# A convolution's backward pass: transposing the gradient in contiguous blocks with a DMA scatter, and leaving out two rows of zeros

## The chip, the cores and the metric

The kernel runs on one core of one Trainium2 chip. The metric is the device time of that core in microseconds (us). "PE" in the profile is TensorE, "PEld" its weight loads, "DVE" VectorE, "ACT" ScalarE, "POOL" GpSimd, "SP" SyncE. L445 is line 445 of the kernel. A line of a group reads: line, engine, operation, tiles (out<-in), shapes, count | busy time in us, mean ns of one | idle time before it and what ended it; a line of a timeline: start, duration, then the same. "From start to start" is the time from the first instruction of a group to the first of the next: matmuls overlap (those of L466 last 273 ns each by the page and are 109.3 ns apart from start to start), so this, and not their durations, adds up to the time. An eviction is the copy of a result out of the PSUM tile that TensorE wrote. The runs were made on several chips of the kind, on which the kernel before took 2769.7 to 2773.3 us, so kernels are compared by their ratio to the kernel before on the same chip. A ratio is the mean time of one kernel's fast runs over that of the other's of the same rounds, so it is not quite the ratio of the medians that are quoted.

## The reference

A strided 1-D convolution (31 taps, stride 2, 256 channels in and out), a normalisation over time per channel, a GELU; the kernel returns the output and all gradients.

```python
B, T, D, K = 2, 16000, 256, 31
L = (T - K) // 2 + 1                                   # 7985
h = sum over i of  x[:, i:i + 2*L:2, :] @ w[i]         # 31 matmuls per output
h = (h - mean_l(h)) / sqrt(var_l(h) + 1e-5) * gn_gamma + gn_beta
out = gelu(h)                                          # tanh form
# returned: out, and by jax.vjp with grad_out: grad x, grad w, grad gn_gamma, grad gn_beta
```

## The kernel before

It runs in stages: forward of both batches (up to some 930 us); transposing the weights while VectorE and ScalarE do the elementwise backward of the second batch (up to 1102); the layout stage; gradient of x (up to 1880); gradient of w (up to 2750). After the elementwise stage the gradient lies in `gu` as channels x time. The gradient of w needs it as time x channels, in `gQ`: partition q holds times 64 q to 64 q + 63. So the layout stage transposes, for each r in 0..63, the 125 columns r, r + 64, r + 128, ...:

```python
R = 64; NQ = 125; NR = R
# phase_gq(b, gate): layout stage
for zr in (0, NR + 1):                                  # a row of zeros before and after
    nc.scalar.activation(out=gQv[:, zr, :], ..., scale=0.0, bias=gate)
for r0 in range(0, NR, 4):
    ptr = ptr_tile()                                    # one PSUM tile, no second buffer
    for rr in range(4):
        r = r0 + rr
        for dc in range(2):
            nc.tensor.transpose(out=ptr[0:NQ, rr * 2 + dc, :],                              # L445
                                in_=guv[:, dc, bass.DynSlice(HALO + r, NQ, step=R)], identity=ident)
    gated_copy(ci % 2 == 1, gQv[0:NQ, 1 + r0:1 + r0 + 4, :], ptr[0:NQ, ...], gate)   # ACT or DVE in turn
```

`gate` is a zero that is known only when the elementwise stage is done. The gradient of w takes two taps (ih, il = ih - 2) at once: one matmul 512 wide with two neighbouring rows of gQ. For r = -1 and r = 63 one of the two rows is a row of zeros.

```python
# phase_bwd_w: gradient of w
for u in range(u_lo, u_hi + 1, 2):                      # u_lo starts at ih - 2
    for pi, (ih, il) in enumerate(pairs):
        r = (u - ih) // 2                               # -1 .. 63
        nc.tensor.matmul(accs[pi][:, 0:2*D], lhsT=chunk[0:nq_u, kk, cc*P:(cc+1)*P],  # L534
                         rhs=gQv[0:nq_u, 1 + r:3 + r, :], start=..., stop=...)
# the end, second batch: load the first batch's partial sum, add, store
for pi, (ih, il) in enumerate(pairs):
    res16 = gwpool.tile(..., name="gwres", bufs=2);  prev = gwpool.tile(..., name="gwprev", bufs=2)
    nc.gpsimd.dma_start(out=prev, in_=gw_scr[...]); nc.vector.tensor_tensor(out=res16, in0=prev, in1=accs[pi], op=ALU.add)
    nc.gpsimd.dma_start(out=out_2[ih, ...], ...);   nc.gpsimd.dma_start(out=out_2[il, ...], ...)
```

## Time and profile before

Median 2769.75 us of 4 runs (2769.6 to 2770.21).

| stage | from, us | to, us | what fills TensorE |
|---|---|---|---|
| forward, two batches | 0 | 931 | L234, 512 wide |
| weights transposed, elementwise stage | 935.0 | 1102 | L598, L380, early blocks of L466 |
| layout | 1102 | 1187.2 | L445, with L466 between |
| gradient of x | 1187.2 | 1880.0 | L466, 256 wide |
| gradient of w | 1880.0 | 2750.2 | L534 512 wide, L539 256 wide |
| end | 2750.2 | 2767.9 | nothing |

Read a row of the profile by its stage: busy time counts in full where TensorE is dense, and may cost nothing where it waits anyway. The lines are in the prediction.

### The profile page before, as it was taken

What the parts mean: (1) busy time and instruction counts of PE and PEld (TensorE: products, weight loads), DVE (VectorE), ACT (ScalarE), POOL (GpSimd) and SP (SyncE); (2) the same over time, 40 slices, a digit from 0 to 9 for tenths busy, and PEclk for the clock granted to TensorE, in tenths of its full rate; (3) what the DMA queues carried; (4) which work ended last, traced back from release to release, by engine and by line L of the source; (5) the groups of instructions that cost most, each with busy time, mean ns of one, the idle gap of its engine ahead of it and who ended that gap; (6) DMA issues with size and microseconds to landing.
All of it is one profiled execution on the core that took longest, in us unless ns stands there. A gap on an engine that the chain in (4) does not pass through costs nothing.

```text
span 2767.9 us, 38654 instructions
## 1 busy us (share of the span) xinstructions
PE 2712.7 (98%) x17351; PEld 1676.5 (61%) x17444; DVE 450.5 (16%) x1105; ACT 402.2 (15%) x785; POOL 263.3 (10%) x464
## 2 busy tenths in 40 slices
PE   8999999999999999999999999999999999999997
PEld 4444445444444678998888888885444454444443
DVE  1000000993000398100000000000000000000000
ACT  1000001964000575200000000000000000000000
POOL 2000000111000011011111111110000000011001
PEclk9999999999999999999999999999999999999998
DMA  5000000112000221000000000002333333333332
GB/s 161 16 24 16 24 13 24 43 53 60 24 16 13 75 72 39 8 18 21 21 21 20 20 20 21 21 21 60 120 99 94 96 119 102 103 114 118 104 109 83
DMA packets 214554, 152.89 MB, mean 55 GB/s; under 512 B 11268, under 2 KB 201392, under 8 KB 214388
## 3 DMA queue, kind: packets, MB, share of 16 engines
q1 hardware_dynamic: 189988, 95.32, 11.6%
q0 software_dynamic: 20368, 53.06, 5.3%
q8 instruction: 136, 2.23, 0.4%
q10 hardware_dynamic: 4032, 2.03, 0.2%
q14 instruction: 30, 0.25, 0.0%
HBM read 113.62 MB, written 36.75 MB: 54 GB/s over the span
## 4 chain that ended last, share of the span: by engine, by line
PE 88%; DVE 8%; ACT 1%; issue 1%; DMA 1%; POOL 0%; SPq 0%; POOLq 0%; ACTq 0%; DVEq 0%
PE acc L534 30%; PE acc L466 27%; PE acc L234 26%; PE ptx L445 2%; DVE etmp L364 1%; DVE gu L366 1%; DVE etmp L368 1%; PE acc L539 1%; DVE etmp L361 1%; PE ptx L196 1%; DVE gu L425 1%; DVE etmp L360 1%; DVE etmp L363 1%; PE pte L312 1%; DMA xn<-in_x_dram 1%
## 5 line engine op out<-in xcount | busy, mean ns | idle before, releaser
L466 PE MATMUL acc<-wB,gu 128*128 128x256 bf16 (+1 forms) x7812 | 870.4, 273 | 1.2 <-issue 1.2
L534 PE MATMUL acc<-gQ,xqc 125*128 125x512 bf16 (+1 forms) x3900 | 870.0, 379 | 0.0
L234 PE MATMUL acc<-xw,w_sb 128*128 128x512 bf16 (+1 forms) x3875 | 860.9, 375 | 6.1 <-issue 1.1
L466 PEld LDWEIGHTS <-gu 128*128 128x128 bf16 (+1 forms) x7812 | 769.4, 99 | 89.4 <-issue 2.9
L534 PEld LDWEIGHTS <-xqc 125*128 125x128 bf16 (+1 forms) x3900 | 380.6, 98 | 434.8 <-issue 0.2
L234 PEld LDWEIGHTS <-w_sb 128*128 128x128 bf16 x3968 | 375.7, 97 | 413.0 <-issue 2.5
L480 POOL DMA_DIRECT2D out_dram<-gxs x252 | 136.0, 540 | 786.6 <-ACT gxs L476 389.0
L478 DVE CAST gxs<-acc 128x256 bf16<-128x256 f32 (+1 forms) x126 | 53.4, 424 | 658.3 <-PE acc L466 656.7
L476 ACT CAST gxs<-acc 128x256 bf16<-128x256 f32 (+1 forms) x126 | 46.7, 371 | 657.6 <-PE acc L466 655.0
L241 ACT ACTIVATE hT<-acc 128x512 bf16<-128x512 f32 (+1 forms) x64 | 37.5, 587 | 651.1 <-PE acc L234 649.6
L200 DVE COPY xw<-ptx 128x1024 bf16<-128x1024 bf16 (+1 forms) x64 | 43.1, 673 | 544.7 <-PE ptx L196 544.7
L561 DVE TENSOR_TENSOR gwres<-gwprev,acc 128x512 bf16<-128x512 f32 (+1 forms) x32 | 20.6, 669 | 413.3 <-PE acc L534 352.8
L549 DVE COPY gwstg<-acc 128x512 f32<-128x512 f32 (+1 forms) x16 | 10.5, 658 | 432.4 <-PE acc L534 373.1
L549 ACT COPY gwstg<-acc 128x512 f32<-128x512 f32 x16 | 9.4, 585 | 436.2 <-PE acc L534 388.7
L391 POOL DMA_DIRECT2D out_dram<-ost x31 | 22.4, 724 | 529.2 <-ACT ost L388 472.7
L539 PE MATMUL acc<-gQ,xqc 125*128 125x256 bf16 x256 | 69.8, 273 | 0.0
L445 PEld LDWEIGHTS <-gu 128*125 128x125 bf16 x256 | 58.3, 302 | 1.3 <-issue 0.9
L555 POOL DMA_DIRECT2D gw_scr<-gwstg x32 | 17.2, 541 | 420.0 <-ACT gwstg L549 414.9
L445 PE MATMUL ptx<-ident,gu 128*125 128x128 bf16 x256 | 54.7, 358 | 1.0 <-DVE gQ L273 0.9
L565 POOL DMA_DIRECT2D out_dram<-gwres x32 | 17.3, 541 | 385.4 <-DVE gwres L561 334.6
L196 PE MATMUL ptx<-ident,xn 128*128 128x128 bf16 x496 | 39.7, 224 | 13.1 <-DMA xn<-in_x_dram 11.4
L353 ACT ACTIVATE etmp<-hT,vec 128x512 bf16<-128x512 bf16 (+1 forms) x64 | 51.2, 799 | 6.3 <-DVE etmp L364 6.0
(98 smaller groups left out, 929.5 us busy)
## 6 DMA issues: line engine op xcount, KB each, us to landing
xqc<-in_x_dram SPq DMA_DIRECT2D x120, 500.0 KB
out_dram<-gxs POOLq DMA_DIRECT2D x248, 64.0 KB, 1.8
xn<-in_x_dram SPq DMA_DIRECT2D x60, 256.0 KB
gnat<-in_grad_out_dram POOLq DMA_DIRECT2D x30, 256.0 KB, 3.1
gw_scr<-gwstg POOLq DMA_DIRECT2D x30, 256.0 KB, 5.6
gwprev<-gw_scr POOLq DMA_DIRECT2D x30, 256.0 KB, 5.6
xqc<-in_x_dram SPq DMA_DIRECT2D x16, 434.0 KB
out_dram<-ost POOLq DMA_DIRECT2D x31, 128.0 KB, 2.2
```

The source lines that it names most:

```text
L196: nc.tensor.transpose(out=ptr[:, bb * NCC + cc, :], in_=xn[:, bi0 + bb, cc * P:(cc + 1) * P], identity=ident[:, :])
L200: nc.vector.tensor_copy(out=dst, in_=src)
L234: nc.tensor.matmul(pst[:, 0:lw], lhsT=w_sb[:, cc, i, dc * P:(dc + 1) * P], rhs=xw[:, p, cc, j:j + lw], start=(k == 0), stop=(k == nmm - 1),)
L241: nc.scalar.activation(out=hTv[:, dc, l0:l0 + lw], in_=pst[:, 0:lw], func=ACT.Identity, accum_out=st.hsum[:, dc, wi:wi + 1])
L353: nc.scalar.activation(out=Tt[:, 0:cw], in_=hs, func=ACT.Square, bias=B_, scale=A_)
L445: nc.tensor.transpose(out=ptr[0:NQ, rr * NDC + dc, :], in_=guv[:, dc, bass.DynSlice(HALO + r, NQ, step=R)], identity=ident[:, :])
L466: nc.tensor.matmul(pso[0:mw, 0:D], lhsT=guv[:, dc, HALO + m0 - j:HALO + m0 - j + mw], rhs=wB[:, dc, i, :], start=(k == 0), stop=(k == nmm ...
L476: nc.scalar.copy(out=gxs[0:mw, :], in_=pso[0:mw, 0:D])
L478: nc.vector.tensor_copy(out=gxs[0:mw, :], in_=pso[0:mw, 0:D])
L480: nc.gpsimd.dma_start(out=dst, in_=gxs[0:mw, :])
L534: nc.tensor.matmul(accs[pi][:, 0:2 * D], lhsT=chunk[0:nq_u, kk, cc * P:(cc + 1) * P], rhs=gQv[0:nq_u, 1 + r:3 + r, :], start=st_flag, stop ...
L539: nc.tensor.matmul(accs[pi][:, 0:D], lhsT=chunk[0:nq_u, kk, cc * P:(cc + 1) * P], rhs=gQv[0:nq_u, 1 + r, :], start=st_flag, stop=sp_flag)
```

## The change

Its intent: read contiguous columns in the transposes, so that they cost what the contiguous transposes of L598 cost (55 ns each, beside 211), and let DMAs do the rearranging (a block of 128 times is two rows of gQ; each half of 64 partitions x 512 bytes is copied into one partition). Spread these sets among the blocks of the gradient of x in a fixed order, one set per six blocks after 48 blocks in free order. And multiply no row of zeros: the first row's second half becomes one 256-wide matmul of its own.

```diff
-        gQv = gQt[:, 0:(NR + 2) * D]...
-        for zr in (0, NR + 1): nc.scalar.activation(... zeros ...)
-        for r0 in range(0, NR, RPT): ...
-                    nc.tensor.transpose(out=ptr[0:NQ, ...], in_=guv[:, dc, bass.DynSlice(HALO + r, NQ, step=R)], ...)
-            gated_copy(ci % 2 == 1, gQv[0:NQ, 1 + r0:1 + r0 + nr, :], src, gate[0:NQ, :])
+        gQv = gQt[:, 0:NR * D]...
+        for k0 in range(0, NBQ, BPT):                     # 63 blocks of 128, four to a set
+            for bb in range(nb): ...
+                    nc.tensor.transpose(out=ptr[0:wdt, ...], in_=guv[:, dc, HALO + l0:HALO + l0 + wdt], ...)
+            stq = stage.tile([P, NBLKCH, D], BF16, name="gnat", bufs=3)
+            gated_copy(ci % 2 == 1, stq[...], ptr[...], None)
+            for bb ...: for qq in range(nqq):             # 8 copies a set, SP and GpSimd in turn
+                    eng.dma_start(out=gQv[q0 + qq:q0 + qq + 1, 0:NR, :], in_=stq[qq * R:(qq + 1) * R, bb, :])
+            yield
 ...
-                f = ih - 2 if il is not None else ih
+                f = ih
-                        if il is not None:                 # 512 wide, rows r and r + 1
+                        if il is not None and r <= NR - 2: # 512 wide; else 256 wide
 ...
+                        if st_flag and has_edge[pi]:       # the first row's second half, 256 wide
+                            nc.tensor.matmul(accs[pi][:, D:2 * D], lhsT=<x of u - 2>, rhs=gQv[0:nq_e, 0, :], start=False, ...)
 ...
-    for b in range(B): phase_gq(b, zdep[B - 1])
-    for b in range(B): phase_bwd_data(b, wB)
+    PACE, FREE = 6, 48
+    for _ in range(FREE): next(blocks)
+    with tc.manual_schedule(engines={PE, Pool, SP, Activation, DVE}):
+        for n, _ in enumerate(blocks):
+            if n % PACE == 0: next(sets, None)
```

## The prediction

> **What bounds the kernel now.** I read the page's busy times first, then the chain of work that ended last, then the costliest groups, then the timeline of the stage that the change rewrites.
>
> ```profile
> PE 2712.7 (98%) x17351; PEld 1676.5 (61%) x17444; DVE 450.5 (16%) x1105; ACT 402.2 (15%) x785; POOL 263.3 (10%) x464
> ...
> PE 88%; DVE 8%; ACT 1%; issue 1%; DMA 1%; POOL 0%; SPq 0%; POOLq 0%; ACTq 0%; DVEq 0%
> ...
> L466 PE MATMUL acc<-wB,gu 128*128 128x256 bf16 (+1 forms) x7812 | 870.4, 273 | 1.2 <-issue 1.2
> L534 PE MATMUL acc<-gQ,xqc 125*128 125x512 bf16 (+1 forms) x3900 | 870.0, 379 | 0.0
> ...
> L539 PE MATMUL acc<-gQ,xqc 125*128 125x256 bf16 x256 | 69.8, 273 | 0.0
> L445 PEld LDWEIGHTS <-gu 128*125 128x125 bf16 x256 | 58.3, 302 | 1.3 <-issue 0.9
> ...
> L445 PE MATMUL ptx<-ident,gu 128*125 128x128 bf16 x256 | 54.7, 358 | 1.0 <-DVE gQ L273 0.9
> ```
>
> TensorE is the bound: 98% busy, and idle before its large groups for about a microsecond in all. Work taken off another engine is worth nothing; what counts is TensorE's issue time. The mean durations (273, 379, 358 ns)[...] cannot be multiplied by counts. The chain gives the true rates, because its long pieces are dense:
>
> ```profile
> 1187.21 692.90 PE acc L466 x6340
> 1880.11 336.82 PE acc L534 x1560
> ```
>
> So a matmul 256 wide (line 466, gradient of x) costs 692.90 / 6340 = 109.3 ns, one 512 wide (line 534, gradient of w) 336.82 / 1560 = 215.9 ns. The layout stage being rewritten (line 445) sits between them, interleaved with line 466:
>
> ```profile
> 1109.11 1.70 PE L445 MATMUL ptx<-ident,gu 128*125 128x128 bf16 x8
> 1110.65 1.36 PE L466 MATMUL acc<-wB,gu 128*128 128x256 bf16 x11
> 1112.02 1.71 PE L445 MATMUL ptx<-ident,gu 128*125 128x128 bf16 x8
> 1113.56 1.04 PE L466 MATMUL acc<-wB,gu 128*128 128x256 bf16 x8
> 1114.57 1.70 PE L445 MATMUL ptx<-ident,gu 128*125 128x128 bf16 x8
> ```
>
> From 1109.11 to 1114.57 are 5.46 us, with 19 matmuls (2.08 us at 109.3 ns) and 16 transposes. The rest is 3.38 us: 211 ns per transpose. The same kernel makes transposes of contiguous columns elsewhere:
>
> ```profile
> 958.88 0.61 PE L598 MATMUL ptx<-ident,xqc 128*128 128x128 bf16 x8
> 959.32 1.48 PE L466 MATMUL acc<-wB,gu 128*128 128x256 bf16 x12
> 960.70 0.61 PE L598 MATMUL ptx<-ident,xqc 128*128 128x128 bf16 x8
> 961.14 0.60 PE L466 MATMUL acc<-wB,gu 128*128 128x256 bf16 x4
> ```
>
> Eight of these take 0.44 us from start to start, 55 ns each. The difference is in the weight load: 302 ns for 125 columns 64 elements apart, against 97 to 99 ns in the groups that load contiguous columns.
>
> [...] The old load has both faults: 125 columns, and a step of 128 bytes. The trace shows the 302 ns but cannot say which fault makes it; the change repairs both. [...] the 64 KB stores of gxs landed in 1.8 us at the median[...].
>
> **The change part by part.**
>
> (a) Layout of the gradient. Removed: 256 strided transposes. In the window 1102.81 to 1187.21 are 84.4 us with 288 matmuls of line 466 (31.5 us), leaving 52.9 us for 31 groups; one group ran earlier, at 966.18, in 1.7 us. Sum 54.6 us of TensorE. Added: 63 blocks x 2 halves x 2 batches = 252 contiguous transposes, in 32 sets. At 55 to 57 ns a set of eight is 0.45 us; in the dense forward stage a window of 28.28 us holds 124 wide matmuls (26.77 us), 16 such transposes and four small ones (about 0.3 us), which makes 0.6 us a set with its switches. I take 0.55 us: 32 x 0.55 = 17.6 us. Saved: 37 us.
>
> (b) What replaces the stride. Each set is evicted into a staging tile (0.75 us on VectorE or 1.11 us on ScalarE, as the old evictions of the same size took) and scattered by 250 small DMAs in all, half on SyncE and half on GpSimd. GpSimd gets 125 x 0.54 us = 67 us more, at the 538 ns of its gxs stores, in a stage of some 800 us where it is 16% busy. The bytes are 8 MB over about 650 us, 12 GB/s beside the 21 now moved. One set comes every six blocks, 6 x 32 x 0.1093 = 21 us, far more than a set's eviction and DMAs need. The 252 blocks leave 204 after the free 48, so 34 places for 32 sets; the last set starts 18 blocks, some 60 us, before the weight gradient needs anything. Cost on the path: none.
>
> (c) Start of the sets. The first scatter needs the slots of the second batch's elementwise stage, which ends at about 1102. By then line 466 has issued 151 + 231 + 389 + 423 = 1194 matmuls, 37 blocks. Forty-eight free blocks reach past that, so the fixed order should not stall. The old gate does cost something:
>
> ```profile
> 1096.36 5.51 PE L466 MATMUL acc<-wB,gu 128*128 128x256 bf16 x49 [1.20 <-issue]
> 1102.81 1.70 PE L445 MATMUL ptx<-ident,gu 128*125 128x128 bf16 x8 [0.94 <-DVE gQ L273]
> 1104.35 2.37 PE L466 MATMUL acc<-wB,gu 128*128 128x256 bf16 x11
> ```
>
> TensorE waits 0.94 us for the first gated eviction, and the next 11 matmuls take 2.17 us from start to start in place of 1.20. Saved: 2 us.
>
> (d) Zero rows in the weight gradient. Now each of 15 pairs runs 65 wide matmuls for each of 2 column halves and 2 batches: 15 x 65 x 4 = 3900, as the page says. The first and last of each multiply a row of zeros. After: 63 wide and two narrow, so 120 wide matmuls become 120 narrow ones: 120 x (215.9 - 109.3) = 12.8 us saved. The narrow ones still hide their weight load, as line 539 does: a row of three wide and one narrow takes 0.755 us at the end (3 x 0.2159 + 0.107).
>
> Forward, elementwise stage, gradient of x (7812 matmuls) and the 18 us after the last matmul stay. Sum: 37 + 12.8 + 2 = 52 us. 2769.75 - 52 = 2718 us, a ratio of 0.981.
>
> **The rivals.** First, contiguous transposes are not at 55 ns here: the weights come from gu, 32 interruptions may each cost a drained pipeline. At 1 us a set the saving in (a) is 22 us and the time 2733 us. For it: during the elementwise stage small groups lost 0.1 to 0.5 us. Against it: most of that was waiting for VectorE's operands, and here operands and PSUM tile are ready some 20 us ahead.
>
> Second, the scatter becomes the wait: single-partition writes land slowly, staging tiles (three) run out, GpSimd stands at a copy with the gxs stores behind it, and accumulators fill up. A few us per set would give all back: 2770 us or over. Against it: 21 us per set for 8 DMAs, and DMA engines 5 to 6% busy. If the fixed order stalls at its head because the slots are not free, it is 10 to 20 us once; the 48 blocks speak against it.
>
> Third, the gain is larger: idle time between 938 and 1187 is about 19 us in sum (249 us less 162 of line 466, 55 of line 445 and about 14 of other transposes); a different order could close 5 more of it. Time 2713 us, just over 2%.
>
> **Range and chances.** 2% is 2714.4 us, only 3.6 us below my number. Run-to-run spread is 0.6 us, so the error is in my terms: +-2 us in the transposes, +-3 us in the elementwise stage's order, and a tail upward for stalls. Eight in ten: 2711 to 2729. Faster by over 2%: 0.23. Within 2%: 0.74. Slower by over 2%: 0.03.
>
> **What would show it.** (a) The new transposes should cost 0.45 to 0.6 us per set from start to start, with weight loads near 100 ns or below. (b) No TensorE idle put down to staging tiles or accumulators from 1102 on; copies land in 2 to 5 us. (c) No gap at the end of the elementwise stage. (d) 3780 wide and 376 narrow matmuls, a weight-gradient stage of about 857 us, was 870. Wrong if line 466 no longer runs at 109.3 ns between sets, if the weight gradient starts late, or if the elementwise stage itself is stretched.

## The result, and the profile after

2714.16 us median of 8 runs (2711.1 to 2715.59), ratio 0.9799 with a 95% interval of 0.9789 to 0.9809. The predicted number was 2718, the range 2711 to 2729: right, and 2.01% is on the line between "within 2%" and "faster", so the verdict at 2% is unclear.

From the changed kernel's page: busy times, the chain that ended last, the groups that answer to L466, L534 and L539 (now L489, L567, L570; the edge matmuls, L575, are 60 more), and the new copies.

```profile
PE 2661.0 (98%) x17347; PEld 1636.4 (60%) x17440; DVE 450.3 (17%) x1107; ACT 398.0 (15%) x781; POOL 329.3 (12%) x588
...
PE 88%; DVE 8%; ACT 2%; DMA 1%; issue 1%; POOL 0%; SPq 0%; POOLq 0%; ACTq 0%; DVEq 0%
...
L489 PE MATMUL acc<-wB,gu 128*128 128x256 bf16 (+1 forms) x7812 | 869.9, 273 | 0.7 <-issue 0.7
...
L567 PE MATMUL acc<-gQ,xqc 125*128 125x512 bf16 (+1 forms) x3780 | 856.1, 379 | 0.0
...
L570 PE MATMUL acc<-gQ,xqc 125*128 125x256 bf16 (+1 forms) x316 | 84.9, 273 | 0.0
...
L472 POOL DMA_DIRECT2D gQ<-gnat x124 | 65.2, 531 | 14.5 <-ACT gnat L266 7.9
```

The bound has not moved: TensorE is still 98% of the span and 88% of the chain, it has only 52 us less to do. GpSimd got 66 us more, all off the path. In the timeline of the changed kernel (start, duration, instruction), a set of transposes and the blocks behind it:

```profile
1143.53 0.61 PE L448 MATMUL ptx<-ident,gu 128*128 128x128 bf16 x8
...
1143.98 21.12 PE L489 MATMUL acc<-wB,gu 128*128 128x256 bf16 x192
...
1164.94 0.61 PE L448 MATMUL ptx<-ident,gu 128*128 128x128 bf16 x8
```

From the first to the second line are 0.45 us: eight transposes at 56 ns, where the old ones took 1.69 (8 x 211 ns). From the second to the third are 20.96 us for 192 matmuls, 109.2 ns each: the blocks go on at full rate between sets. The stages of both traces, each from a first start to the next:

| piece | before, us | after, us | saved |
|---|---|---|---|
| start to first weight transpose | 935.0 | 936.0 | -1.0 |
| weight transposes to gradient of w | 945.0 | 904.1 | 40.9 |
| gradient of w to its last matmul | 870.2 | 857.2 | 13.0 |
| last matmul to the end | 17.7 | 15.7 | 2.0 |
| span | 2767.9 | 2713.0 | 54.9 |

The 40.9 us of the second row are the layout (54.6 - 32 x 0.44 = 40.5) and 0.4 for everything else in it; the clock has a part in that 0.4, see (c) below.

### The profile page after: what moved, and what is told of

Read it like the earlier page. It is cut to its first block, busy times and chain, and to the rows that moved or that the text cites. A ratio compares the mean times of both kernels' runs of the same rounds, so it can differ in the third digit from the quotient of the medians.

```text
span 2713.0 us, 39137 instructions
## 1 busy us (share of the span) xinstructions
PE 2661.0 (98%) x17347; PEld 1636.4 (60%) x17440; DVE 450.3 (17%) x1107; ACT 398.0 (15%) x781; POOL 329.3 (12%) x588
## 4 chain that ended last, share of the span: by engine, by line
PE 88%; DVE 8%; ACT 2%; DMA 1%; issue 1%; POOL 0%; SPq 0%; POOLq 0%; ACTq 0%; DVEq 0%
PE acc L567 30%; PE acc L489 28%; PE acc L234 26%; PE acc L570 1%; DVE etmp L364 1%; DVE gu L366 1%; DVE etmp L368 1%; DVE etmp L361 1%; PE ptx L196 1%; DMA xn<-in_x_dram 1%; DVE etmp L360 1%; DVE etmp L363 1%; PE pte L312 1%; DVE etmp L358 1%; PE ptx L448 1%
## 5 line engine op out<-in xcount | busy, mean ns | idle before, releaser
L489 PE MATMUL acc<-wB,gu 128*128 128x256 bf16 (+1 forms) x7812 | 869.9, 273 | 0.7 <-issue 0.7
L567 PE MATMUL acc<-gQ,xqc 125*128 125x512 bf16 (+1 forms) x3780 | 856.1, 379 | 0.0
L489 PEld LDWEIGHTS <-gu 128*128 128x128 bf16 (+1 forms) x7812 | 764.1, 98 | 89.3 <-issue 2.6
L567 PEld LDWEIGHTS <-xqc 125*128 125x128 bf16 (+1 forms) x3780 | 369.0, 98 | 412.5 <-issue 0.2
L570 PE MATMUL acc<-gQ,xqc 125*128 125x256 bf16 (+1 forms) x316 | 84.9, 273 | 0.0
L583 DVE COPY gwstg<-acc 128x512 f32<-128x512 f32 (+1 forms) x16 | 10.5, 658 | 426.3 <-PE acc L570 366.3
L472 POOL DMA_DIRECT2D gQ<-gnat x124 | 65.2, 531 | 14.5 <-ACT gnat L266 7.9
L196 PEld LDWEIGHTS <-xn 128*128 128x128 bf16 x496 | 33.8, 100 | 29.8 <-DMA xn<-in_x_dram 13.0
```

The costliest lines, as they stand in the source:

```text
L196: nc.tensor.transpose(out=ptr[:, bb * NCC + cc, :], in_=xn[:, bi0 + bb, cc * P:(cc + 1) * P], identity=ident[:, :])
L472: eng.dma_start(out=gQv[q0 + qq:q0 + qq + 1, 0:NR, :], in_=stq[qq * R:(qq + 1) * R, bb, :])
L489: nc.tensor.matmul(pso[0:mw, 0:D], lhsT=guv[:, dc, HALO + m0 - j:HALO + m0 - j + mw], rhs=wB[:, dc, i, :], start=(k == 0), stop=(k == nmm ...
L567: nc.tensor.matmul(accs[pi][:, 0:2 * D], lhsT=lhsT, rhs=gQv[0:nq_u, r:r + 2, :], start=st_flag, stop=sp_flag)
L570: nc.tensor.matmul(accs[pi][:, 0:D], lhsT=lhsT, rhs=gQv[0:nq_u, r, :], start=st_flag, stop=sp_flag)
```

## The experiments

Twelve kernels ran. Three (6, 7 and 12) gave an answer of another size than I had written down, and the probe of shapes (4) overthrew both simple reasons for the slow transposes.

**1 and 2. Each part alone.** First the kernel before with only the zero rows left out (the edits of the second part of the diff, with gQ still holding its zero rows); then the changed kernel with the zero rows put back (the first and third part of the diff).

> The kernel before with part (d) alone: the zero rows are no longer multiplied, the layout stage stays strided. My theory: TensorE time is additive, so 120 wide matmuls that become narrow save 120 x 106.6 ns = 12.8 us: about 2757 us, ratio 0.9954. Rival (the weight gradient is bound by its loads of x, or the edge matmuls on the previous chunk drain the pipeline): less than 6 us saved, over 2763 us. Also to be read here: whether the end after the last matmul is 18 us, as in the kernel before, or 16 us, as in the changed one.

> The changed kernel with the zero rows put back: parts (a), (b), (c) alone. My theory: the layout saves 54.6 - 13.8 = 40.8 us and the gate under 1 us, so about 2728 us, ratio 0.985, and with the rows-only kernel the two savings add up to that of the whole change. Rival (the two parts share something, as a common end or a common wait): the sum of the two savings differs from 55 us by more than 4 us.

Rows alone: 2761.15 us beside 2772.99, ratio 0.9957 (0.9945 to 0.9970), 12 us. Layout and order alone: 2728.2 us, ratio 0.9840 (0.9827 to 0.9854), 44 us. The sum is 56 us, the whole change gave 56 us. Each saving is known to some 3 or 4 us by its interval; within that the two parts are additive, as one expects where one engine, here TensorE with 98% of the span busy, is the bound throughout.

**3. Is it the step?** The kernel before with one edit:

```diff
-  in_=guv[:, dc, bass.DynSlice(HALO + r, NQ, step=R)]
+  in_=guv[:, dc, HALO + r:HALO + r + NQ]
```

> The kernel before with one edit: the transposes of the layout stage read 125 neighbouring columns in place of 125 columns 64 apart. The result is wrong on purpose; count, place and evictions of the transposes stay. If the step makes the slow weight load, a transpose falls from 211 to some 55 to 60 ns and the time to about 2730 us, and the scatter and the fixed order are only there to pay for contiguous reads. If the 125 columns (not a full 128) make it, little changes: over 2755 us. A third way: TensorE then outruns the single PSUM tile and its evictions of 0.75 and 1.11 us, and gives part back as waits: 2735 to 2745 us.

2736.72 us, ratio 0.9873 (0.986 to 0.9887): 36 us saved with the old order, the old evictions and 125 columns. In its trace eight transposes take 0.46 us from start to start, and after the first (2.58 us) no eviction held TensorE:

```profile
1104.37 0.62 PE L445 MATMUL ptx<-ident,gu 128*125 128x128 bf16 x8 [2.58 <-DVE gQ L273]
1104.83 1.36 PE L466 MATMUL acc<-wB,gu 128*128 128x256 bf16 x11
```

256 x (211 - 57) ns would be 39.4 us; the rest went into longer waits: 2.58 us for the first gated eviction, where the kernel before had 0.94, and 2.96 in the pause before it, where the kernel before had 1.20. So a step of 1 is enough. The experiment does not say that the step is the fault by itself.

**4. Which shapes are slow.** The changed kernel with eight more transposes ahead of each set, whose result the right ones overwrite:

```diff
+            pstep, pcols = PROBE[k0 // BPT]
+            for j in range(TRW):
+                nc.tensor.transpose(out=ptr[0:pcols, j, :],
+                                    in_=guv[:, j % NDC, bass.DynSlice(HALO + j // NDC, pcols, step=pstep)], identity=ident)
```

> The changed kernel with eight more transposes ahead of each set, into the same PSUM tile, which the right ones then overwrite: in each batch 16 shapes, of 128 or 125, 127 or 64 columns and steps of 1 to 64 elements. To be read per group of eight from start to start. Line theory[...]: the same time for 125, 127 and 128 columns; at 128 columns flat at 0.44 us for a step of 1, growing up to a step of 8 (16 bytes), then flat at 1.7 us. Column theory[...]: 125 and 127 columns are slow at a step of 1 too[...] and 128 columns 62 apart are near 0.44 us. The changed kernel is longer by the sum, some 25 to 35 us.

2741.01 us (one run), 26 us above the profiled run of the changed kernel, 24 by the ratio on this run's chip. The timeline of this run: the second set's probe (125 columns, step 64), the third's (125 columns, step 1), and the fourth's (128 columns, step 62); L455 are the right transposes behind each.

```profile
1166.12 1.81 PE L447 MATMUL ptx<-ident,gu 128*125 128x128 bf16 x8
1167.76 0.61 PE L455 MATMUL ptx<-ident,gu 128*128 128x128 bf16 x8
...
1189.17 0.62 PE L447 MATMUL ptx<-ident,gu 128*125 128x128 bf16 x8
1189.63 0.61 PE L455 MATMUL ptx<-ident,gu 128*128 128x128 bf16 x8
...
1210.38 0.68 PE L447 MATMUL ptx<-ident,gu 128*128 128x128 bf16 x8
1210.90 0.61 PE L455 MATMUL ptx<-ident,gu 128*128 128x128 bf16 x8
```

From start to start: 1.64, 0.46 and 0.52 us. The line theory blames the step, the column theory the width; both fall in their simple form. The line theory wanted 128 columns with a step of 62 slow; the column theory wanted 125 contiguous columns slow. Slow is only what has both faults.

**5. The edges.** The same probe with other shapes.

> The probe of shapes again with others, to find the edges. At 125 columns steps 2 to 8: the first probe had 2 fast (0.48 us per eight) and 8 slow (1.78). Line theory[...]: slow grows with the step and is full[...] at 8; a step of 4 would be near 0.9 us. Switch theory: a jump at one step. At a step of 62: 127, 126 and 112 columns as slow as 125 (1.7 us)[...], and 96, 64, 32 falling with the number of columns (64: 0.9 us); the same time for all widths if the cost is not per column.

The timeline of this run, for a step of 8 at 125 columns, then a step of 62 at 128 and at 127 columns:

```profile
1274.41 1.94 PE L447 MATMUL ptx<-ident,gu 128*125 128x128 bf16 x8
1276.18 0.61 PE L455 MATMUL ptx<-ident,gu 128*128 128x128 bf16 x8
...
1296.28 0.68 PE L447 MATMUL ptx<-ident,gu 128*128 128x128 bf16 x8
1296.80 0.61 PE L455 MATMUL ptx<-ident,gu 128*128 128x128 bf16 x8
...
1316.90 1.94 PE L447 MATMUL ptx<-ident,gu 128*127 128x128 bf16 x8
1318.67 0.61 PE L455 MATMUL ptx<-ident,gu 128*128 128x128 bf16 x8
```

One column fewer makes 0.52 us into 1.77. Both probes together, us per eight transposes from start to start (each shape came twice, the two within 0.02 us):

| columns | step 1 | 2 | 3 | 4 | 5 | 6 | 7 | 8 | 16 | 62 to 64 |
|---|---|---|---|---|---|---|---|---|---|---|
| 128 | 0.45 | 0.45 | | 0.44 | | | | 0.49 | 0.50 | 0.52 (62) |
| 125 | 0.46 | 0.47 | 0.67 | 0.88 | 1.10 | 1.33 | 1.54 | 1.77 | 1.80 | 1.64 (64) |

At a step of 62: 127 columns 1.77, 126 columns 1.76, 112 columns 1.57, 96 columns 1.33, 64 columns 1.07, 32 columns 0.63. Also: 127 columns 0.47 at a step of 1 and 1.81 at 8; 64 columns 0.57 at a step of 1 and 0.63 at 4; 125 columns 1.70 at 63; 128 columns 0.50 at 32. So with 125 columns the cost rises by some 0.22 us a step, from a step of 2 to one of 8 (0.47 us to 1.77), and hardly further (1.80 at 16, 1.64 at 64); at a step of 62 it falls with the columns below 128 (1.77 at 127, 0.63 at 32); with exactly 128 columns a step of up to 62 adds at most 0.08 us (0.44 to 0.52). How the steps from 1 to 8 cost at other widths than 125 was hardly tested. The line theory gave the slope and its end, the column theory the switch; what in the load makes them is not shown.

**6. The cure with three columns.** The kernel before, right result, gu padded so that the strided transposes can read 128 columns:

```diff
-    GW = HALO + max(R * NQ, max(MP)) + 2
+    GW = HALO + max(R * P, max(MP)) + 2
-  out=ptr[0:NQ, ...], in_=guv[:, dc, bass.DynSlice(HALO + r, NQ, step=R)]
+  out=ptr[:, ...],    in_=guv[:, dc, bass.DynSlice(HALO + r, P, step=R)]
```

> The kernel before with the strided transposes kept, 64 elements apart, but reading 128 columns in place of 125 (gu is padded for it; the three extra rows are not evicted). Right result. After the probe I think that the slow weight load needs both faults at once: at 128 columns a step of 62 cost 0.52 us per eight, at 125 columns a step of 1 cost 0.46, at 125 with a step of 64 1.64. Then a transpose costs 65 ns, 256 x 146 ns = 37 us saved, less the 3 us more that the run with step 1 lost at the gate: about 2738 us on a chip where before is 2772, ratio 0.988. Rival (a step of 64 elements, a power of two, is slow by itself, 62 is not): little change, ratio over 0.995.

2744.33 us beside 2770.32, ratio 0.9904 (0.9890 to 0.9917): 27 us saved, where I wrote 34. The rival, that a step of 64 is slow by itself, is wrong, but 64 is not 62: eight transposes take 0.66 us here, 83 ns each, with a median weight load of 193 ns.

```profile
1110.13 0.81 PE L445 MATMUL ptx<-ident,gu 128*128 128x128 bf16 x8
1110.78 1.36 PE L466 MATMUL acc<-wB,gu 128*128 128x256 bf16 x11
```

256 x (211 - 83) ns = 33 us, less what the gate took again (2.49 us for the first eviction), and some microseconds that I did not trace. Why 64 costs 0.14 us more than 62 is open.

**7. Does the scatter cost anything?** The changed kernel's order and rows, but these 128-column transposes evicted straight into gQ, no staging and no copies:

> The changed kernel with its order and without its zero rows, but with the 128-column strided transposes evicted straight into their place: no staging, no scatter of 250 copies. If the scatter is hidden, as I think, the time is that of the changed kernel plus 32 x 0.08 us = 2.6 us: ratio 0.981 against before. If the scatter costs something that I do not see, this is faster than the changed kernel: ratio under 0.978.

2727.65 us, ratio 0.9843 (0.9829 to 0.9856): some 12 us slower than the changed kernel by the ratios, not 2.6. Its sets take 0.67 us in place of 0.44, 32 x 0.23 = 7 us. The rest is not the transposes': in its profile the weight transposes start at 939.7 us, not 936.0, for a reason that I did not trace, and the stretch from the last issue on GpSimd to the end is 9.5 us, not 7.5. (The two profiled runs are 10.5 us apart: between these two places its trace is only 4.9 us longer than the changed kernel's, and 6.8 longer than that of experiment 11, which has the same order.) So the scatter is hidden at this pace, and contiguous reading is worth 7 us over the padded strided form, by the times of the sets.

**8 to 10. How much room the order has.** The changed kernel with one line edited: `PACE, FREE = 1, 48`, then `2, 48`, then `6, 16`.

> The changed kernel with a set after every block in place of every sixth: a set every 3.9 us. In the profile of the changed kernel the copies of one set (eight, 32 KB each, into eight neighbouring partitions) land 8 us after issue[...], and three staging tiles are in use. If what fills the 8 us is latency, three sets in flight fit a set every 3.9 us and the time stays within 3 us of the changed kernel. If it is the rate at which a few partitions take bytes (256 KB a set[...]), the staging tiles run out and TensorE stands: 32 x (1 to 5) us = 30 to 160 us more.

> The changed kernel with a set every two blocks, 7.4 us. Latency theory: same time as the changed kernel. Rate theory at 5 us a set: same; at 9 us a set: 32 x 1.6 = 50 us more. With the run of every block this brackets the time of a set's scatter.

> The changed kernel with 16 free blocks in place of 48, so that the first set comes some 75 us before the elementwise stage of the second batch gives up the slots that the scatter writes. If the head of the fixed order stalls (my step c), GpSimd and SyncE stand at the first copies, gxs stores queue behind them and TensorE stops until 1102: 10 to 60 us more. If the slots do not matter, the same time within 2 us.

One run each, beside a kernel before of 2773.32 us, at which the changed kernel's ratio gives 2717.6. A set after every block: 2771.07, 53 us lost. Every second block: 2719.43, nothing that one run shows. Sixteen free blocks: 2757.31, 40 us lost. TensorE's waits in the first of these (us in total, times, longest), and how long GpSimd's half of the copies took in the changed kernel itself:

```profile
PE ptx L448 <- DVE gnat L268: 22.8, 11, 3.5
PE ptx L448 <- ACT gnat L266: 17.0, 8, 4.3
```

```profile
DMA to landing us min/median/max: 5.2/8.1/9.0
```

TensorE waits for the PSUM tile, whose eviction waits for a staging tile, which waits for the copies. With a set at every block the 32 sets start from 1146.05 to 1316.87, 5.5 us apart on average: 256 KB in 5.5 us is 48 GB/s. The latency theory, by which the time stays within 3 us, falls; the rate theory fits: at this pace GpSimd's copies land after up to 16.2 us, not 9.0 (median 7.9, beside 8.1). The room at six blocks (21.4 us a set) is fourfold. What sets the rate is not shown; the DMA engines were 82% busy from 1146 to 1320 us, where the changed kernel, at a set per 21.4 us, has 31% (1143 to 1790 us). The two waits sum to 39.8 of the 53 us; the granted clock was 0.94 in the same 174 us (0.990 over the run, 0.995 in the changed kernel), which is worth up to 10 more (an estimate, 0.06 x 174). In the run with 16 free blocks GpSimd's waits hold this line:

```profile
POOL gQ L472 <- ACT etmp L422: 74.9, 1, 74.9
```

GpSimd stood 74.9 us at the first copy, until the elementwise stage gave up the slot that the copy writes; the stores of the gradient of x queued behind it, and TensorE ran short of accumulators: it waited 16.6 us at once for an eviction of the gradient of x, and before that had little but the elementwise stage's own transposes to do (27.1 us of waits for their operands, 8.0 in the changed kernel), with the granted clock at 0.50 from 1051 to 1078 us (0.68 over 1050 to 1100).

**11 and 12. A shorter end.** After the last matmul the changed kernel waits for two partial sums, in its chain of waits (start, us, what):

```profile
2700.39 2.94 DMA gwprev<-gw_scr
...
2703.41 0.70 DVE gwres L595
```

The buffers for these are two, so the last two loads can only be issued when the first two additions are done. The edits, on the changed kernel and on the one of experiment 7:

```diff
-  name="gwres", bufs=2 ... name="gwprev", bufs=2
+  name="gwres", bufs=4 ... name="gwprev", bufs=4
-  for pi, (ih, il) in enumerate(pairs):
+  for pi, (ih, il) in reversed(list(enumerate(pairs))):      # in the order in which they finish
-  nc.gpsimd.dma_start(out=out_2[ih, ...])
+  (nc.sync if <last group> else nc.gpsimd).dma_start(out=out_2[ih, ...])
```

> The changed kernel with its last 16 us shortened: four buffers in place of two for the partial sums loaded back and for the results, the pairs finished in the order in which their matmuls end, and the last stores split over two queues. The wait of 4.84 us for two loads goes, and three of four additions move ahead of the last matmul: 5 to 8 us less than the changed kernel, ratio 0.977 to 0.978. If the end is bound by the last stores and the teardown, under 2 us.

> Both: strided transposes of 128 columns without scatter, in the changed kernel's order, and the shorter end. Additive theory: 2.6 us over the run with the shorter end alone, ratio 0.978 to 0.979; below both kernels of the study if the end gives over 2.6 us.

The changed kernel with the shorter end: 2706.12 us, ratio 0.9768 (0.9754 to 0.9781), faster than both kernels, by over 2% against the kernel before and by 8.5 us against the changed one, a little more than I wrote; in the traces 7.3 of that lie behind the last matmul (15.7 us, now 8.4). VectorE's additions in its timeline:

```profile
2693.43 0.42 DVE L595 TENSOR_TENSOR gwres<-gwprev,acc 128x256 bf16<-128x256 f32 x1 [45.21 <-PE acc L570]
...
2694.62 2.04 DVE L595 TENSOR_TENSOR gwres<-gwprev,acc 128x512 bf16<-128x512 f32 x3 [0.77 <-PE acc L570]
```

They follow TensorE's last matmuls one by one; no load is waited for. The other: 2720.44 us, ratio 0.9818 (0.9804 to 0.9831), 7 us under experiment 7 and 14 above the one before it, where I wrote 2.6; so again the copies beat the padding, and again part of it is a later start (938.9 us against 936.3) and a longer end.

## Why the prediction was right, point by point

**What bounds the kernel**: right. The time followed TensorE's issue time; the chain is PE's for 88% before and after.

**(a) The layout**: the mechanism was right, a size was off. The term "I take 0.55 us" for a set, which added switches to eight transposes of 55 ns, measured 0.44 to 0.45: in this trace, with operands and PSUM tile ready, switching costs nothing that shows beside the 55 to 56 ns of each transpose. This is 3.5 us of the 4 that the number was too high. The prediction left open which of the two faults makes the load slow; experiments 4 and 5 show that it takes both, and experiment 6 that three more columns cure most of it (211 ns to 83).

**(b) The scatter**: "cost on the path: none" was right, "copies land in 2 to 5 us" was wrong: 8.1 us at the median for GpSimd's half. It is not a fixed time per copy: of a batch's last set, which has five copies and not eight, GpSimd's two landed after 5.5 us (issued at 1785.5 us). So it seems that the copies of a set hold each other up; where is not shown. Rival two describes what happens at six times the pace; at this pace it does not.

**(c) The start of the sets**: that 48 blocks reach past the elementwise stage was right, and experiment 10 shows the stall that would come otherwise. "Saved: 2 us" rests on a misreading. The wait of 0.94 us for the gated eviction is gone. But the 11 matmuls behind it (2.17 us in place of 1.20, 197 ns each in place of 109) were not slow by the gate's wait: the trace of the kernel before has a granted clock of 0.50 from 1104.5 to 1107.9 us, and 1.00 after it. Experiments 1 and 6 show such a stretch at the same place; experiment 3, whose wait at the gate is as long as theirs, shows 1.00 there. These matmuls also lie in the 54.6 us of (a), so they were counted twice. In the changed kernel's trace the clock is 1.00 at that place, but an earlier stretch of 0.50 is 6.8 us long (976.8 to 983.6), where the kernel before has 3.4 (978.2 to 981.6). So the 0.4 us is the figure of one trace: in the traces of experiments 2 and 11, which have the same order and 3.4 us there, this piece takes 902.4 and 902.2 us, not 904.1, and the rest of it gives some 2 us. What sets these stretches is open. The pause some 6 us before the gated eviction, which I showed beside it, is still there in the changed kernel's timeline:

```profile
1097.51 14.75 PE L489 MATMUL acc<-wB,gu 128*128 128x256 bf16 x132 [0.75 <-issue]
```

The profile names only "issue" as what ends it, so its cause stays open; the gate it was not.

**(d) Zero rows**: 12.8 us predicted, 13.0 in the trace, 12 by experiment 1.

**Not foreseen**: 2.0 us after the last matmul. It lies behind the last issue on GpSimd: 9.5 us to the end in the kernel before and in experiments 1, 3, 6 and 7, 7.5 to 8.6 in the changed kernel and the kernels with copies of experiments 2, 4, 5 and 8 to 10. It goes with the scatter, not with the order; why, the profile does not show. The start of the second part, 1.0 us later, goes the other way. That the number came out within 4 us is in part luck: these errors of 1 to 2 us, and that of (c), have opposite signs.

**Rivals**: the first (1 us a set) is wrong, the second needs a tighter order, the third (the gain is larger, 2713) was nearest in size but not in reason: TensorE's waits for the elementwise stage did not shrink (8.4 us in all, before 8.0).

## What to carry to other kernels

Where one engine is 98% busy, add up start-to-start times of its instructions, not their mean durations; here the sum held to 4 us in 2700. Before blaming a wait for slow instructions behind it, read the granted clock of that stretch (here 0.50 from 1104.5 to 1107.9 us, where 11 matmuls took 2.17 us in place of 1.20). Here a strided weight load was slow at 127 columns and not at 128 (1.77 and 0.52 us per eight transposes at a step of 62): try padding the width before building a way around the stride. The DMA scatter into neighbouring partitions was free here at a set per 21.4 us and cost 53 us where a set was asked for after every block; find the pace at which it is not, and look at what its first copy waits for before fixing an order around it.
